# Banded QK scores of a dilated attention: from products on VectorE to dense blocks on TensorE

## The chip, the cores and the metric

The kernel runs on one core of a Trainium2 chip. The metric is the device time of one execution in microseconds. The core has TensorE (PE, matrix products into PSUM), VectorE (DVE), ScalarE (ACT), GpSimd (POOL) and SyncE (SP), whose queue issues nearly all DMAs here. Each engine takes its instructions in order; semaphores tie them together.

## The reference

Two branches work on the same x (2048 positions, 1024 channels) and are mixed by a gate. Branch A is an attention with 32 heads of 32 channels in which every position looks at itself and at the seven positions 2, 4, ... 14 before it. Branch B is a gated MLP whose gate is mixed over positions by a 2048 x 2048 matrix.

```python
g = sigmoid((x * gate_w).sum(-1, keepdims=True))

# A: W = 8 keys per query, dilation 2
q, k, v = split(x @ wqkv)                      # 32 heads x 32 channels
idx = pos[:, None] - 2 * arange(8)[None, :]    # keys of a position; idx < 0 is masked
logits = einsum('bhsd,bhswd->bhsw', q, k[idx]) * 32 ** -0.5
a = einsum('bhsw,bhswd->bhsd', softmax(where(idx >= 0, logits, -1e9)), v[idx]) @ wo

# B
z = gelu(x @ w_in)                             # 2048 x 3584
z1, z2 = z[..., :1792], layernorm(z[..., 1792:])
b = (z1 * (w_sp @ z2 + b_sp[:, None])) @ w_out

out = g * a + (1 - g) * b
```

## The kernel before

One arena in SBUF is cut into regions that are used again from stage to stage (Z, X, A, CD, EF by their offsets); the tile framework sets the semaphores and orders each engine's instructions from the program order and from priorities (`tc.high_priority()` lifts a piece). PSUM is eight banks of 512 words a partition, handed out in turn by `next_bank`. The stages, in the order in which TensorE does them:

1. Start: x is brought in transposed (`xT`), and a first quarter of z2 (`z2_tile(i, 0)`, L214) with the gate's column is made. `g_d` and `og_d` carry the gate through DRAM.
2. QKV: for each of eight groups of four heads, 16 tiles `j` (L249). A tile takes the positions j, j+16, j+32, ... as its rows, so its weights are read from `xT` at a stride, and gives q, k and v of the group side by side, 384 columns. ScalarE copies it to a stage slot (L252), and every fourth tile three DMAs write q, k and v to `q_d`, `k_d` and `v_d`. The weights of v are first reordered on ScalarE (L244).
3. Attention, VectorE only, group by group: q, k and v come back from DRAM so that a partition holds 16 consecutive positions and the 14 before them (`q_t`, `k_t`, `v_t`). In two halves of eight positions, q times the eight shifted k (L273, 8192 products a partition), four halving adds over the 32 channels (L276) and a last one into `att_L` (L277), then the mask (L278), the softmax in 32 bits (L279 to L290) with the exponential on ScalarE (L283), the products with v (L295) and three halving adds over the eight keys (L297 to L299). Every second group is written to `o_d`.
4. The other three quarters of z2 (L214), its layer norm (L311 to L322), then z1 (L381), which goes to `z1_d` over two slots (`z1s_slots`).
5. Spatial product: the 2048 x 2048 product as two halves of seven `spatial_quad` each, and within these seven products of half size in the manner of Strassen, each of eight matmuls (L391); the sums of operands are VectorE's. The two halves of w_sp are read by DMA transposes (`load_raw`, eight each; SP's line L187). The second half's place, `raw_slots[1]`, is at `A_OFF`, where `q_t`, `k_t`, `v_t`, `prod` and `obuf` of the attention lie.
6. Output: eight `out_quad`, seven products of eleven matmuls (L391), from `zg_d` and `o_d`.

The framework lets the attention on VectorE run beside stages 2, 4, 5 of TensorE; work of the spatial stage with high priority goes between its instructions.

Of the kernel before, what the change touches and what calls it, by code (L numbers as in the profile page):

```python
# [28 lines left out]
NEG = -1.0e30  # L29
EPS = 1e-5  # L30
SCALE = DH ** -0.5
WGS = 4 * KT * C
# [19 lines left out]
def kernel(  # L52
# [32 lines left out]
    def reg(off, n):  # L85
        return arena[:, off:off + n]

    q_d = dpool.tile([NG, S, C], BF, name="q_d")
    k_d = dpool.tile([NG, S + 16, C], BF, name="k_d")
# [9 lines left out]
    mask = sm.tile([P, 2 * W * 8 * HG], BF, name="mask")  # L99
    nc.gpsimd.memset(mask[:], 0.0)  # L100
    m5 = mask[:].rearrange("p (a w j h) -> p a w j h", a=2, w=W, j=8, h=HG)
    for jh in range(2):
        for w in range(W):
            n = min(8, max(0, 14 - 2 * w - 8 * jh))
            if n > 0:
                nc.gpsimd.memset(m5[0:1, jh, w, 0:n, :], NEG)
# [14 lines left out]
    att_L = sm.tile([P, 2 * W * 8 * HG], F32, name="att_L")  # L121
    att_m = sm.tile([P, 2, 4, 32], F32, name="att_m")
    att_r = sm.tile([P, 2, 1, 32], F32, name="att_r")
    att_A = sm.tile([P, 2 * W * 8 * HG], BF, name="att_A")

# [6 lines left out]
    q_t = reg(A_OFF, NJ * C)  # L132
    k_t = reg(A_OFF + 2048, NJJ * C)
    v_t = reg(A_OFF + 2048 + 3840, NJJ * C)
    prod = reg(A_OFF + 2048 + 7680, W * 8 * C)
    obuf = reg(A_OFF + 2048 + 7680 + 8192, NJ * 2 * C).rearrange("p (j c) -> p j c", j=NJ)
    w2 = reg(CD_OFF, KT * W2P).rearrange("p (k c) -> p k c", k=KT)
    w2_off = [0, 480, 480 + ZC, 480 + 2 * ZC]
    stage_slots = [reg(CD_OFF + 14848 + r * 1536, 1536).rearrange("p (j c) -> p j c", j=4) for r in range(3)]
    wg_slots = [reg(EF_OFF + r * WGS, WGS).rearrange("p (t k c) -> p t k c", t=4, k=KT) for r in range(3)]  # L140
    junk = reg(EF_OFF + 3 * WGS, FH)
# [17 lines left out]
    def load_wg(g, dma):  # L159
        wgt = wg_slots[g % 3]  # L160
        dma(wgt[:, 3, :, :], wq_v[:, :, 2 * D + g * C:2 * D + (g + 1) * C])
        dma(wgt[:, 0, :, :], wq_v[:, :, g * C:(g + 1) * C])
        dma(wgt[:, 1, :, :], wq_v[:, :, D + g * C:D + (g + 1) * C])
# [8 lines left out]
    load_wg(0, lambda o, i: chained(nc.sync.dma_start(o, i)))  # L172
    load_wg(1, lambda o, i: chained(nc.sync.dma_start(o, i)))
    for t_d in (k_d, v_d):
        chained(nc.sync.dma_start(bass.AP(tensor=t_d.tensor, offset=t_d.offset, ap=[[16, P], [(S + 16) * C, NG], [1, 16]]), zeros[:]))
# [34 lines left out]
    def z2_tile(i, c):  # L210
        N = ZC + 1 if c == 0 else ZC
        ps = next_bank()
# [18 lines left out]
    sync.dma_start(g_att[:], bass.AP(tensor=g_d.tensor, offset=g_d.offset, ap=[[NJ, P], [1, NJ]]))  # L231

    stg = 0
    for g in range(NG):
        wgt = wg_slots[g % 3]
        if g > 1:
            load_wg(g, sync.dma_start)
        vdst = wgt[:, 2, :, :].rearrange("p k (d h) -> p k d h", d=DH, h=HG)
        vsrc = wgt[:, 3, :, :].rearrange("p k (h d) -> p k d h", h=HG, d=DH)
        if g == 0:  # L240
            nc.scalar.copy(vdst[:, 0:4], vsrc[:, 0:4])
            nc.vector.tensor_copy(vdst[:, 4:8], vsrc[:, 4:8])
        else:
            nc.scalar.copy(vdst, vsrc)  # L244
        for j in range(NJ):
            ps = next_bank()
            for kt in range(KT):
                lhsT = _sub_ap(xT_flat, kt * S + j, [[NJ, P]])
                nc.tensor.matmul(ps[:, 0:3 * C].rearrange("p (t c) -> p t c", t=3), lhsT, wgt[:, 0:3, kt, :],  # L249
                                 start=(kt == 0), stop=(kt == KT - 1))  # L250
            st = stage_slots[stg % 3]
            nc.scalar.copy(st[:, j % 4, :], ps[:, 0:3 * C])  # L252
            if j % 4 == 3:
                j0 = j - 3
                dq = bass.AP(tensor=q_d.tensor, offset=q_d.offset + (g * S + j0) * C, ap=[[NJ * C, P], [C, 4], [1, C]])
                dk = bass.AP(tensor=k_d.tensor, offset=k_d.offset + (g * (S + 16) + 16 + j0) * C, ap=[[NJ * C, P], [C, 4], [1, C]])
                dv = bass.AP(tensor=v_d.tensor, offset=v_d.offset + (g * (S + 16) + 16 + j0) * C, ap=[[NJ * C, P], [C, 4], [1, C]])
                sync.dma_start(dq, st[:, :, 0:C])
                sync.dma_start(dk, st[:, :, C:2 * C])
                sync.dma_start(dv, st[:, :, 2 * C:3 * C])  # L260
                stg += 1

    L = att_L
    L4 = L[:].rearrange("p (a w n) -> p a w n", a=2, w=W, n=32)
    A4 = att_A[:].rearrange("p (a w n) -> p a w n", a=2, w=W, n=32)
    for g in range(NG):
# [3 lines left out]
        for jh in range(2):  # L270
# [4 lines left out]
            for half in (16, 8, 4, 2):  # L275
                nc.vector.tensor_tensor(pv[:, :, 0:half], pv[:, :, 0:half], pv[:, :, half:2 * half], ALU.add)  # L276
# [29 lines left out]
    for c in range(1, 4):  # L306
        sync.dma_start(w2[:, :, w2_off[c]:w2_off[c] + ZC], win_v[:, :, FH + ZC * c:FH + ZC * (c + 1)])
    for i in range(16):
        for c in range(1, 4):
            z2_tile(i, c)  # L310
# [314 lines left out]
```

## Time and profile before

| | us |
|---|---|
| median of 2 runs (766.35 to 766.77) | 766.56 |
| the profiled execution | 767.75 |
| its span, first to last instruction | 765.7 |
| busy TensorE / VectorE / ScalarE | 683.0 / 527.4 / 247.9 |
| mean granted TensorE clock | 0.958 |
| moved by DMA | 108.15 MB |

The profile is of one execution. A group of its lines is a line of the kernel, an engine, an operation and its operands, the count, the busy time and the mean of one in ns, then the engine's idle time just before them and what ended it. A matmul's shown duration overlaps the next one's, so tiles are better read from the distance of their starts. A stage's length is read from TensorE's timeline: 37.7 us start, 185.2 QKV, 80.4 rest of z2, about 101 z1, 361.4 spatial and output.

### The profile page before, as it was taken

The page shows a single profiled execution, that of the slowest core. Times are in us where ns is not written, and L with a number is a line of the kernel's source. Part 1 is how long each engine was busy: PE and PEld are TensorE (multiplying, and loading weights), DVE is VectorE, ACT ScalarE, POOL GpSimd, SP SyncE. Part 2 cuts the span into 40 slices and gives each one's busy share as a digit, 9 for nine tenths or more (in the row PEclk, how much of TensorE's full clock was granted, in tenths as well). Part 3 has the DMA queues.
Part 4 walks back from the last instruction along what each step waited for, and adds up shares of the span by engine and source line. Part 5 has one row for each costly group of instructions (what it writes and reads, how often), then busy time and mean ns, then how long its engine had stood idle before and what let it go on. Part 6 is the DMA issues. An engine that isn't in the chain of part 4 may idle for free.

```text
span 765.7 us, 8952 instructions
## 1 busy us (share of the span) xinstructions
PE 683.0 (89%) x3416; PEld 384.6 (50%) x3416; DVE 527.4 (69%) x559; ACT 247.9 (32%) x502; POOL 13.3 (2%) x23
## 2 busy tenths in 40 slices
PE   5996999999798997989996999910999989999998
PEld 3584888888674553434442444400344434444443
DVE  1000399999999999999999999991587667433300
ACT  3442545252354957325341122200121111222121
POOL 0000000000000011100000000000000000000000
PEclk9997999999999999999998999965899999999999
DMA  9999966646673230993664223289544568964111
GB/s 216 181 97 151 288 162 152 173 103 171 160 188 135 90 96 2 206 306 117 190 212 134 55 71 95 70 250 203 110 110 134 147 133 173 206 134 101 46 42 42
DMA packets 246362, 108.15 MB, mean 141 GB/s; under 512 B 206896, under 2 KB 237616, under 8 KB 246320
## 3 DMA queue, kind: packets, MB, share of 16 engines
q1 hardware_dynamic: 245280, 107.59, 58.0%
q8 instruction: 26, 0.43, 0.3%
q10 hardware_dynamic: 1040, 0.00, 0.1%
q14 instruction: 16, 0.13, 0.1%
HBM read 56.11 MB, written 35.73 MB: 120 GB/s over the span
## 4 chain that ended last, share of the span: by engine, by line
DVE 42%; PE 32%; DMA 10%; SPq 9%; issue 4%; ACT 2%; POOL 1%; DVEq 0%; ACTq 0%; POOLq 0%
DVE arena L276 8%; DVE arena L273 7%; DVE arena L295 6%; PE bank_68 L391 4%; PE bank_72 L391 4%; PE bank_74 L391 4%; DVE arena L297 4%; PE bank_71 L391 4%; SPq L187 4%; PE bank_67 L391 4%; PE bank_70 L391 4%; SPq L171 3%; DMA g_d<-g_s 2%; PE bank_69 L391 2%; DMA arena<-z_d 2%
## 5 line engine op out<-in xcount | busy, mean ns | idle before, releaser
L391 PEld LDWEIGHTS <-arena 128*128 128x128 f16 (+1 forms) x1400 | 138.5, 99 | 219.2 <-issue 51.0
L249 PEld LDWEIGHTS <-arena 128*128 128x128 bf16 x1024 | 148.1, 145 | 36.1 <-issue 17.2
L273 DVE TENSOR_TENSOR arena<-arena 128x8192 bf16<-128x8192 bf16 x16 | 70.8, 4426 | 46.6 <-DMA arena<-k_d 46.3
L391 PE MATMUL bank_71<-arena 128*128 128x512 bf16 x200 | 49.2, 391 | 34.1 <-DMA arena<-in_B_w_sp_dram 34.1
L214 PEld LDWEIGHTS <-arena 128*128 128x128 bf16 x512 | 50.9, 100 | 55.8 <-issue 11.1
L276 DVE TENSOR_TENSOR arena<-arena 128x4096 bf16<-128x4096 bf16 (+1 forms) x64 | 77.6, 1212 | 1.4
L381 PEld LDWEIGHTS <-arena 128*128 128x128 bf16 x448 | 43.8, 98 | 56.9 <-issue 4.4
L295 DVE TENSOR_TENSOR arena<-arena,att_A 128x8192 bf16<-128x8192 bf16 x16 | 70.8, 4424 | 0.4
L391 PE MATMUL bank_70<-arena 128*128 128x512 f16 x200 | 48.7, 388 | 5.0 <-DVE arena L420 5.0
L391 PE MATMUL bank_72<-arena 128*128 128x512 f16 x200 | 48.5, 388 | 3.4 <-ACT bank_72 L399 2.7
L391 PE MATMUL bank_68<-arena 128*128 128x512 f16 x200 | 48.3, 386 | 2.4 <-DVE arena L421 2.4
L391 PE MATMUL bank_67<-arena 128*128 128x512 bf16 x200 | 48.5, 387 | 0.0
L391 PE MATMUL bank_74<-arena 128*128 128x512 f16 x200 | 46.7, 379 | 1.7 <-DVE arena L363 1.7
L420 DVE TENSOR_TENSOR arena<-arena 128x1024 f16<-128x1024 f16 (+2 forms) x30 | 17.9, 602 | 36.2 <-DMA arena<-zg_d 13.8
L297 DVE TENSOR_TENSOR arena<-arena 128x4096 bf16<-128x4096 bf16 x16 | 36.6, 2290 | 0.3
L399 ACT COPY bank_72<-bank_71 128x512 f32<-128x512 f32 x11 | 6.3, 570 | 84.4 <-PE bank_71 L391 71.0
L249 PE MATMUL bank_71<-arena 128*128 128x384 bf16 x128 | 24.7, 338 | 7.4 <-ACT arena L252 7.4
L422 DVE TENSOR_TENSOR arena<-arena 128x1024 f16<-128x1024 f16 (+2 forms) x30 | 17.7, 602 | 16.6 <-PE bank_72 L391 8.4
L249 PE MATMUL bank_67<-arena 128*128 128x384 bf16 x128 | 24.7, 338 | 4.3 <-ACT arena L252 4.3
L311 ACT ACTIVATE arena<-arena 128x1792 bf16<-128x1792 bf16 x16 | 27.2, 1700 | 0.4
L283 ACT ACTIVATE att_L<-att_L 128x512 f32<-128x512 f32 x8 | 5.0, 630 | 65.1 <-DVE att_L L282 65.1
L249 PE MATMUL bank_69<-arena 128*128 128x384 bf16 x128 | 23.4, 326 | 1.5 <-ACT arena L252 1.5
(167 smaller groups left out, 904.1 us busy)
## 6 DMA issues: line engine op xcount, KB each, us to landing
arena<-k_d SPq DMA_DIRECT2D x8, 960.0 KB, 6.7
arena<-v_d SPq DMA_DIRECT2D x8, 960.0 KB, 5.4
z_d<-arena SPq DMA_DIRECT2D x14, 512.0 KB, 5.9
arena<-z_d SPq DMA_DIRECT2D x28, 256.0 KB, 3.3
zg_d<-arena SPq DMA_DIRECT2D x56, 128.0 KB, 2.2
arena<-zg_d SPq DMA_DIRECT2D x32, 224.0 KB, 3.2
arena<-in_A_wqkv_dram SPq DMA_DIRECT2D x24, 256.0 KB, 4.6
q_d<-arena SPq DMA_DIRECT2D x32, 128.0 KB, 5.2
```

Source lines behind the costliest of these rows:

```text
L171: chained(nc.sync.dma_start_transpose(xT[:, :, i * P:(i + 1) * P], x2[i * P:(i + 1) * P, :]))
L187: inst = _orig_dmat(*a, **k)
L214: nc.tensor.matmul(ps[:, 0:N], xT[:, kt, i * P:(i + 1) * P], w2[:, kt, w2_off[c]:w2_off[c] + N], start=(kt == 0), stop=(kt == KT - 1))
L249: nc.tensor.matmul(ps[:, 0:3 * C].rearrange("p (t c) -> p t c", t=3), lhsT, wgt[:, 0:3, kt, :], start=(kt == 0), stop=(kt == KT - 1))
L273: nc.vector.tensor_tensor(prod.rearrange("p (w j c) -> p w j c", w=W, j=8, c=C), in0, in1, ALU.mult)
L276: nc.vector.tensor_tensor(pv[:, :, 0:half], pv[:, :, 0:half], pv[:, :, half:2 * half], ALU.add)
L295: nc.vector.tensor_tensor(prod.rearrange("p (w j d h) -> p w j d h", w=W, j=8, d=DH, h=HG), in0, in1, ALU.mult)
L297: nc.vector.tensor_tensor(p3[:, 0:4, :], p3[:, 0:4, :], p3[:, 4:8, :], ALU.add)
L311: nc.scalar.activation(junk, z2[:, i, :], ACT.Square, accum_out=s2[:, i:i + 1])
L381: nc.tensor.matmul(ps[:], w1[:, kt, (f % 4) * P:(f % 4 + 1) * P], xT[:, kt, 512 * c:512 * (c + 1)], start=(kt == 0), stop=(kt == KT - 1))
L391: nc.tensor.matmul(bank[:], lhsT, rhs, start=(start and m == 0), stop=(stop and m == n - 1), skip_group_check=True)
L420: nc.vector.tensor_tensor(s_out[0], a21, a22, ALU.add)
```

## The change

The scores q·k are no longer made on VectorE. Positions are split by parity, so that the eight keys of a query are eight neighbours within its parity.

- q and k are made transposed (`qk_tile`: channels on partitions, 512 positions a tile) and copied to `qT` and `kT` with even and odd positions apart. v is made for four groups at once (`v_tile`, 512 columns) and reordered in the copy.
- A block is 128 queries of one parity against 135 keys (their own 128 and the 7 before). For each of four heads it is one matmul with 32 channels of contraction; the four heads stand in four row tiles of the array (`tile_position`) and go to banks 4 to 7. Six `band_set` of two or three blocks make a group's 16 blocks. ScalarE copies each head's bank to 16 bits, heads innermost, and a DMA writes the whole rows (135 x 4 values, 1080 bytes) to `band_d`. The part in front of position 0 is filled with -60000 once.
- In `attend`, two DMAs read back, for every query, the 8 x 4 values of its band (64 bytes); the address moves by a row and one key from query to query (`BR + HG`), and that takes the diagonal out. The softmax is in 16 bits. The products with v stay on VectorE.
- Order: q and k of group g+1 (and v in groups 0 and 3, and twelve tiles of z2 in the last) are put between the six sets of group g; these use banks 0 to 3 (`low_bank`). The loads of w2 and of the first two w1 are issued earlier.

```diff
+KW = P + W - 1
+BR = KW * HG
+BS = P * (BR + HG)
...
-    q_d = dpool.tile([NG, S, C], BF, name="q_d")
-    k_d = dpool.tile([NG, S + 16, C], BF, name="k_d")
+    band_d = [dpool.tile([16, BS], F16, name=f"band_d{g}") for g in range(NG)]
...
-    load_wg(0, lambda o, i: chained(nc.sync.dma_start(o, i)))
-    load_wg(1, lambda o, i: chained(nc.sync.dma_start(o, i)))
+    load_wqk(0, lambda o, i: chained(nc.sync.dma_start(o, i)))
+    for hf in range(2):
+        chained(nc.sync.dma_start(wv[:, :, 512 * hf:512 * hf + 512], wq_v[:, :, 2 * D + 512 * hf:2 * D + 512 * hf + 512]))
+        load_wqk(1 + hf, lambda o, i: chained(nc.sync.dma_start(o, i)))
...
-    sync.dma_start(g_att[:], bass.AP(tensor=g_d.tensor, offset=g_d.offset, ap=[[NJ, P], [1, NJ]]))
+    for e in range(2):
+        sync.dma_start(g_att[:, 8 * e:8 * e + 8].rearrange("p (j o) -> p j o", o=1),
+                       bass.AP(tensor=g_d.tensor, offset=g_d.offset + e, ap=[[NJ, P], [2, 8], [1, 1]]))
...
+    def qk_tile(g, t, c):
+        ps = low_bank()
+        w = wqk_slots[g % 4]
+        for kt in range(KT):
+            nc.tensor.matmul(ps[:], w[:, t, kt, :], xT[:, kt, 512 * c:512 * (c + 1)], start=(kt == 0), stop=(kt == KT - 1))
+        dst = (qT_slots, kT_slots)[t][g % 2]
+        nc.scalar.copy(dst[:, :, 256 * c:256 * (c + 1)], ps[:].rearrange("p (n e) -> p e n", e=2))
+
+    def v_tile(hf, j):
...
+        nc.scalar.copy(_sub_ap(st, (j % 4) * 512, [[C, 4], [1, HG], [HG, DH]]), ps[:].rearrange("p (g h d) -> p g h d", g=4, h=HG))
...
+    band_sets = [(0, 8, 2), (1, 1, 3), (9, 1, 3), (4, 1, 3), (12, 1, 3), (7, 8, 2)]
...
+    def band_set(g, x):
+        first, step, n = band_sets[x]
+        qt, kt_ = qT_slots[g % 2], kT_slots[g % 2]
...
+            st = band_slots[band_at[0] % 3]
...
+        for m in range(n):
+            e, b = divmod(first + m * step, 8)
+            for h in range(HG):
+                hp = slice(DH * h, DH * (h + 1))
+                nc.tensor.matmul(banks[4 + h][:, m * KW + lo:(m + 1) * KW], qt[hp, e, P * b:P * (b + 1)],
+                                 kt_[hp, e, P * b - (W - 1) + lo:P * (b + 1)], start=True, stop=True,
+                                 tile_position=(DH * h, 0), skip_group_check=True)
+        for h in range(HG):
+            src = banks[4 + h][:, 0:n * KW].rearrange("p (m k) -> p m k", m=n)[:, :, lo:KW]
+            nc.scalar.copy(st[:, 0:n, lo:KW, h], src)
+        bd = band_d[g]
+        dst = bass.AP(tensor=bd.tensor, offset=bd.offset + first * BS, ap=[[BR, P], [step * BS, n], [1, BR]])
+        sync.dma_start(dst, st[:, 0:n].rearrange("p m k h -> p m (k h)"))
+
+    def attend(g):
+        L = att_L[g % 2]
...
+        for e in range(2):
+            sync.dma_start(L[:, 256 * e:256 * e + 256].rearrange("p (j x) -> p j x", j=8),
+                           bass.AP(tensor=bd.tensor, offset=bd.offset + 8 * e * BS, ap=[[8 * (BR + HG), P], [BR + HG, 8], [1, W * HG]]))
...
-            nc.vector.tensor_tensor(prod.rearrange("p (w j c) -> p w j c", w=W, j=8, c=C), in0, in1, ALU.mult)
-            pv = prod.rearrange("p (n d) -> p n d", d=DH)
-            for half in (16, 8, 4, 2):
-                nc.vector.tensor_tensor(pv[:, :, 0:half], pv[:, :, 0:half], pv[:, :, half:2 * half], ALU.add)
-            nc.vector.tensor_tensor(L[:, jh * 256:(jh + 1) * 256], pv[:, :, 0], pv[:, :, 1], ALU.add)
-        nc.vector.tensor_tensor(L[:], L[:], mask[:], ALU.add)
...
+    for g in range(NG):
+        if g + 3 < NG:
+            load_wqk(g + 3, sync.dma_start)
+        main = []
+        if g in (0, 3):
+            main += [lambda j=j, hf=g // 3: v_tile(hf, j) for j in range(NJ)]
+        if g + 1 < NG:
+            main += [lambda t=t, c=c, g=g + 1: qk_tile(g, t, c) for t in range(2) for c in range(4)]
+        else:
+            main += [lambda c=c, i=i: z2_tile(i, c, low_bank) for i in range(4) for c in range(1, 4)]
+        done = 0
+        for x in range(6):
+            band_set(g, x)
+            upto = (x + 1) * len(main) // 6
+            for m in range(done, upto):
+                main[m]()
+            done = upto
+        attend(g)
...
+    load_w1(0)
+    load_w1(1)
     load_raw(0)
```

In the changed kernel the copies out of the bands are L280, those of q and k L245 and of v L253, the band matmuls L275, those of q and k L243 and of v L250, the exponential L300.

## The prediction

> **What bounds the kernel now.** I read the page's busy times and slices first, then the busy time by stage, then TensorE's one long wait and its releaser, then the costliest groups. In the slices a digit is tenths busy in 19.1 us.
>
> ```profile
> PE 683.0 (89%) x3416; PEld 384.6 (50%) x3416; DVE 527.4 (69%) x559; ACT 247.9 (32%) x502; POOL 13.3 (2%) x23
> PE   5996999999798997989996999910999989999998
> DVE  1000399999999999999999999991587667433300
> ```
>
> TensorE (PE) is the busiest, but VectorE (DVE) is solid from 82 to 520 us. The stages, by time (stretch, length, then busy time and count of each engine):
>
> ```profile
> 37.70:222.90 185.20, 171.97 (x1032) 148.64 (x1031) 129.39 (x96) 72.45 (x154) 0.00 (x0) 0.96 0.74 162
> 222.90:303.30 80.40, 73.32 (x379) 37.35 (x378) 76.06 (x80) 56.33 (x124) 4.94 (x2) 0.98 0.31 97
> 303.30:405.80 102.50, 98.68 (x458) 44.58 (x456) 97.15 (x80) 41.92 (x76) 6.53 (x2) 1.00 0.68 193
> 405.80:520.00 114.20, 86.86 (x386) 38.19 (x384) 110.20 (x131) 17.79 (x30) 0.00 (x0) 0.90 0.41 115
> 520.00:555.00 35.00, 18.37 (x70) 7.47 (x71) 11.14 (x8) 2.88 (x5) 0.00 (x0) 0.71 0.77 165
> 555.00:615.00 60.00, 60.00 (x279) 27.19 (x278) 42.07 (x59) 10.63 (x19) 0.00 (x0) 1.00 0.48 125
> 615.00:765.70 150.70, 144.48 (x661) 64.88 (x659) 58.51 (x100) 29.86 (x52) 0.00 (x0) 0.99 0.50 111
> ```
>
> These are QKV (L249), the rest of z2 (L214), z1 (L381), then the spatial and output products (L391). TensorE is full in all but two, 405.8 to 555, where it idles some 44 of 149 us. The cause is one chain, read from three engines' timelines and the list of waits:
>
> ```profile
> 518.13 0.69 DVE L299 TENSOR_TENSOR arena<-arena 128x1024 bf16<-128x1024 bf16 x1
> 518.85 0.59 SPq L182 DMA_DIRECT2D o_d<-arena  x1
> 519.49 22.91 SPq L187 DMA_TRANSPOSE arena<-in_B_w_sp_dram  x8
> PE bank_71 L391 <- DMA arena<-in_B_w_sp_dram: 34.1, 1, 34.1
> ```
>
> The last attention instruction ends at 518.8. The second half of w_sp (load_raw(1)) is laid over the attention's buffers, so its eight transposes start only then, and TensorE waits 34.1 us for them. So attention on VectorE (43.5 us a group, from 132.17, where a group's first L273 starts, to 175.70, where the next one's does; eight groups) bounds the middle, TensorE's own work the rest.
>
> **TensorE without waits, before.** The timeline's starts give a tile of eight matmuls as 1.30 us at 384 columns, 1.52 at 448 and 1.73 at 512; eleven of 512 take 2.375. z1 is 56 x 1.73 = 96.9. The spatial stage is 14 x 7 x 1.73 = 169.5 and the output 8 x 7 x 2.375 = 133.0, together 302.5, where the trace has 361.4 (404.3 to 765.7): 59 lost.
>
> **Part 1: attention on VectorE, removed.** The costliest groups:
>
> ```profile
> L273 DVE TENSOR_TENSOR arena<-arena 128x8192 bf16<-128x8192 bf16 x16 | 70.8, 4426 | 46.6 <-DMA arena<-k_d 46.3
> L276 DVE TENSOR_TENSOR arena<-arena 128x4096 bf16<-128x4096 bf16 (+1 forms) x64 | 77.6, 1212 | 1.4
> L295 DVE TENSOR_TENSOR arena<-arena,att_A 128x8192 bf16<-128x8192 bf16 x16 | 70.8, 4424 | 0.4
> L244 ACT COPY arena<-arena 128x1024 bf16<-128x1024 bf16 x7 | 14.1, 2013 | 2.0 <-DMA arena<-in_A_wqkv_dram 2.0
> L252 ACT CAST arena<-bank_71 128x384 bf16<-128x384 f32 x16 | 7.9, 496 | 31.6 <-DMA v_d<-arena 25.9 <-PE bank_71 L249 5.7
> ```
>
> L273, L276, L277 (16 x 0.61) and L278 (8 x 0.69) go: 70.8 + 77.6 + 9.7 + 5.5 = 163.6 us. What stays of a group is the value product, 2 x (4.42 + 2.29 + 1.23 + 0.69 + four gaps of 0.035) = 17.5, and the softmax, 5.05 in 32 bits (153.11 to 158.16). In 16 bits I take 4.2, since L276's 512 and 1024 elements already run at half the price of the 32-bit rows. So a group takes 21.7 us (22.6 if 16 bits give nothing). Eight are 174 against 348.
>
> **Part 2: TensorE's projections, moved.** QKV was 128 x 1.30 = 166.4. Now 64 q and k tiles and 32 v tiles of 512 columns take 96 x 1.73 = 166.1, no change. Twelve z2 tiles (18.2 us) move into the stage; 36 (54.7) stay behind it.
>
> **Part 3: band matmuls, added.** 8 groups x 16 blocks x 4 heads = 512 of 135 columns, in 48 sets. No row has this shape. By L381's rate (216 ns per 512 columns) one takes 57 ns, I take 60: 30.7 us. If the four heads truly overlap it is a quarter, 7.7. The worst row is the start's transposes, 128 columns with a weight load each, every 107 ns: 54.8. I stay with 60: right behind those transposes a z2 tile still took 3.21 us against 1.68 for the later ones, so they ran in a slow start.
>
> They also use another tiling of the array (tile_position), so each set changes it twice. No row shows such a change. At the least it costs nothing; at the most the array empties each time, and as a L249 matmul is shown for 326 ns while the next starts after 162, that is 164 ns: 96 x 0.164 = 15.7. I take the middle, 8, since in the sets with one tile between them TensorE waits for banks anyway. The Trainium skill (TensorEngine Tiling (Array Packing), Tiling Modes, Key Properties) says that changing the tiling mode drains TensorE; no row here shows a switch. By the rule the sum has up to all of the 15.7, 8 more; by the row, where matmul follows matmul without a break, none of it, 8 less.
>
> **Part 4: copies out of PSUM on ScalarE (ACT).** Per group 16 of 405 and 8 of 270 elements; before, L252 moved 384 in 496 ns, one every 0.375 us. By that, a set's four end 3 x 0.395 + 0.51 = 1.7 us after they start. The next set (own banks per head) can't finish before: 0.1 wait, nine matmuls 0.54, 0.3 until the copy starts, so 2.6 us a set against 1.73 + 0.72 = 2.45 on TensorE. That costs 0.15 x 4 sets x 6 groups, 4 us. The copies of q, k and v tiles (0.57 each by L401's 512 elements, the v ones permuted) lie under matmul tiles of 1.73 and cost nothing; without that cover the 32 of v are 18 us. Band copies write at a distance of 8 bytes. L244, which reads at 64 bytes, takes 2013 ns for 1024 and L241 1082 for 512, so 1.8 ns an element: 405 would be 0.88. I take L252's price, because the source is PSUM as there.
>
> The Trainium skill (SBUF — State Buffer, Door 1: The DMA port swizzle) says accesses keep full speed with two or more in a 16-byte line. L244 has one, and pays; the new writes have two, so by the rule they are free and by the row 24 x 0.35 = 8 us of ScalarE a group dearer. No row here has two.
>
> **Part 5: the way through DRAM.** A group writes 2.2 MB of bands (six DMAs) where q and k wrote 1.0 and read 1.5. At some 22 us a group, with values (0.96), weights (0.5) and outputs (0.5), that is 4.2 MB / 22 = 190 GB/s; 40:80 us of the start ran at a share of 0.98, 200:240 moved 159 GB/s at 0.57. So it fits. SP issues eleven DMAs a group there at 0.4 to 0.6 us, before 18. The mask's memsets (POOL, 1.9 us in the first 40) and the earlier w1 loads I cost at nothing, because TensorE has z2 work then; bare, one w1 load is 8.1 us. The hand-over per group is write (zg_d's 128 KB land in 2.2 us, z_d's 512 KB in 5.9: 4 for 270 KB), wait and issue 1, read of 2 x 1024 pieces of 64 bytes (896 pieces of zg_d land in 3.2: 3.5), issue 1.5 in all: 10 us, then 1.5 of max and subtract. Ends: 6 by two rows of 2.2, or 16 if the read takes the 9.6 us that g_att's did.
>
> Here is the new wait. The exponential (L300) stands in ScalarE's queue in front of band copies, and TensorE waits for those banks. In the changed kernel's instruction order exp of group 0 stands after group 1's first set (8.7 us after its last band copy), of group 3 after four q/k copies (7.5), others two or three sets on (10 to 13). Ready at 11.5, or when VectorE has finished the group before. Group 0 waits 11.5 + 1.28 for the function table + 0.63 - 8.7, some 4; group 3 11.5 + 0.63 - 7.5, again 4; following both queues the same way through the others (period 20.5 on TensorE, 21.7 on VectorE) gives 1, 1, 0, 0 and 3 for groups 1, 2, 4, 5 and 6, the last with two table loads. SP also blocks: L(4)'s read stands behind an o_d write that waits for attend(3); I count it inside these. Add 2 at the start, where g_att waits for g_d (17.5 us to land) in front of the first band and value writes.
>
> **Sum.** Stage: 166.1 + 18.2 + 30.7 + 8 + 4 + 13 + 2 = 242. It runs from 37.7 to 279.7. Rest of z2, 54.7 + 2: to 336.4. VectorE ends attention near 315, so both halves of w_sp load from there: 16 transposes x 2.5 us on SP (519.49 above: 22.9 for eight), to some 360. The z1 writes stand behind them; two z1 slots and eight banks cover 28 us of TensorE from 336, so 6 are lost: 96.9 + 6. Spatial and output 302.5, and 7 at their two joints (before: 5.0 and 2.4 at 405 to 417, 2.7 at 620), and 3.5 at the end (L565 and the last store). That is 336.4 + 102.9 + 313 = 752.3 of span. The profiled execution took 767.75 with a span of 765.7, 2.05 around it; the median of the runs is 766.56. So **755 us**, of itself 738 to 770.
>
> **Rivals.** *A, the array overlaps and the hand-over is short.* Four heads at once save 23, but then the copies bind (2.4 against 2.6), so 12; short hand-overs save the 9 of groups 0, 1 and 3: 755 - 21 = 734. For it: the tiles name separate row groups and banks. Against: ScalarE.
>
> *B, slower: ScalarE's copies become the bound.* Place: L280. At 0.88 instead of 0.39 us, a group's ScalarE work is 16 x 0.88 + 8 x 0.62 + 8 x 0.57 + 0.6 = 24.2, and with the 0.9 us of turn-round in four sets 28: 7.5 above my 20.5 in six groups, 45: 800. It decides beyond 782 from about 0.7 us a copy. For it L244; against it L252.
>
> *C, the hand-over is long.* At 16 us each of seven groups waits 4 to 6 more: 785 to 797; at 13, some 775. For it the many 64-byte pieces; against, DMA is not full after 120 us.
>
> *D, that the 34 us stay.* Nothing else holds the attention's buffers; no more than 3 in 100, within C.
>
> **How the numbers follow.** Forecast 0.50 (0.20 of it below 751), A 0.20, B 0.17, C 0.13 (half of it within 2%). Two per cent of 766.56 is 15.3 us, about what a measurement of this kernel can tell from no change: faster, under 751.2, 0.20 + 0.20 = 0.40; same 0.30 + 0.07 = 0.37; slower, over 781.9, 0.17 + 0.06 = 0.23. The range goes from A, 730, to short of B's full price, 793, leaving some 2 in 10 out.
>
> **What would show it.** Right: no wait of L391 for w_sp, TensorE full from 340 us, VectorE's attention ending near 315, L280 at 0.5 us, the band matmuls 60 ns apart, ScalarE waiting for VectorE at L300. Wrong: L280 over 0.7 (B), the att_L read over 8 us to landing (C), a stage ending after 300 us, or a new idle stretch at z1 over 15 us.

## Result and the profile after: slower, and ScalarE's copies are the reason

| | us |
|---|---|
| median of 2 runs of the changed kernel (785.79 to 787.84) | 786.82 |
| median before | 766.56 |
| ratio, with its 95% interval | 1.026 (1.021 to 1.032) |
| the profiled execution / its span | 787.84 / 785.7 |

The change costs 20 us where 12 less had been forecast. In the forecast, rival B had named this outcome and its place, L280. The page's busy times and slices (a digit is now tenths of 19.6 us):

```profile
PE 720.4 (92%) x3672; PEld 335.9 (43%) x3672; DVE 361.6 (46%) x462; ACT 402.9 (51%) x649; POOL 6.0 (1%) x13
PE   5997868799778887899999999999999999999998
DVE  1000027487192756795120008667888478332310
ACT  3456968999699889998523332212211121222221
```

VectorE was relieved as meant (527.4 to 361.6 us). But ScalarE rose from 247.9 to 402.9, and its 8s and 9s (slices 5 to 19, 78 to 373 us) lie over the stretch in which TensorE shows 6 to 8 (slices 4 to 17, with two 9s). From slice 18 on TensorE is full. By stage (stretch, length, then busy time and count of PE, PEld, DVE, ACT, POOL, granted clock, DMA share, GB/s):

```profile
37.70:105.20 67.50, 59.58 (x320) 31.45 (x318) 0.25 (x2) 47.57 (x59) 0.00 (x0) 0.92 0.84 148
105.20:292.50 187.30, 152.55 (x897) 67.64 (x896) 112.44 (x110) 165.27 (x215) 0.00 (x0) 0.89 0.47 135
292.50:380.50 88.00, 79.53 (x450) 40.09 (x450) 57.73 (x69) 80.32 (x156) 4.00 (x3) 0.98 0.49 132
380.50:478.40 97.90, 96.78 (x449) 43.79 (x448) 14.13 (x18) 34.07 (x59) 1.01 (x1) 1.00 0.61 154
478.40:785.70 307.30, 302.70 (x1401) 136.91 (x1399) 174.81 (x256) 60.11 (x105) 0.00 (x0) 1.00 0.47 117
```

These are the start with v and group 0, groups 1 to 6, the last group and the rest of z2, z1, and the spatial and output products. In the second row TensorE lacks 35 of 187 us, while ScalarE is busy 88% of it. The last row took 361.4 us before. Of the 54 us that it lost, 34.1 are the wait for w_sp: among TensorE's waits there is none for it any more. The costliest groups of ScalarE, shapes apart:

```profile
L280 ACT CAST arena<-bank_73 128x405 f16<-128x405 f32 x32 | 37.9, 1186 | 0.0
L253 ACT CAST arena<-bank_69 128x512 bf16<-128x512 f32 x8 | 11.6, 1450 | 0.0
L245 ACT CAST arena<-bank_67 128x512 bf16<-128x512 f32 x16 | 9.6, 598 | 13.2 <-PE bank_67 L243 13.2
```

All three copy PSUM into 16 bits. L245 reads PSUM at a distance of 8 bytes and writes in a row: 598 ns for 512. L253 and L280 read in a row and write at 8 bytes: 1450 ns for 512, 1186 for 405. So the price follows the writing side. ScalarE's timeline in the middle, and what TensorE did then (start, duration):

```profile
216.10 0.84 ACT L280 CAST arena<-bank_74 128x256 f16<-128x256 f32 x1
216.67 0.69 ACT L245 CAST arena<-bank_68 128x512 bf16<-128x512 f32 x1
217.49 1.07 ACT L280 CAST arena<-bank_71 128x405 f16<-128x405 f32 x1
218.29 1.18 ACT L280 CAST arena<-bank_72 128x405 f16<-128x405 f32 x1
219.19 1.18 ACT L280 CAST arena<-bank_73 128x405 f16<-128x405 f32 x1
220.10 1.18 ACT L280 CAST arena<-bank_74 128x405 f16<-128x405 f32 x1
221.05 0.65 ACT L245 CAST arena<-bank_69 128x512 bf16<-128x512 f32 x1
```

```profile
208.45 1.90 PE L243 MATMUL bank_68<-arena 128*128 128x512 bf16 x8
215.27 0.21 PE L275 MATMUL bank_71<-arena 32*128 32x135 bf16 x1 [4.92 <-ACT arena L280]
215.84 0.27 PE L275 MATMUL bank_72<-arena 32*128 32x135 bf16 x1 [0.35 <-ACT arena L280]
216.41 0.27 PE L275 MATMUL bank_73<-arena 32*128 32x135 bf16 x1 [0.31 <-ACT arena L280]
216.99 0.27 PE L275 MATMUL bank_74<-arena 32*128 32x135 bf16 x1 [0.31 <-ACT arena L280]
217.42 3.60 PE L243 MATMUL bank_69<-arena 128*128 128x512 bf16 x8
```

```profile
217.40:221.00 3.60, 3.60 (x14) 1.10 (x12) 3.60 (x1) 3.51 (x4) 0.00 (x0) 0.50 0.22 77
```

The starts of successive copies are 0.80, 0.90 and 0.91 us apart: 0.91 is the sustained price, 2.25 ns an element. The four heads' matmuls, which want to start together, start one by one as L280 frees their banks. TensorE also runs slower here: after its stop of 4.92 us the granted clock was 0.50 from 217.4 to 221.0 us, and a tile of q or k took 3.53 us from its start to the next set instead of 1.73. ScalarE was busy 3.51 of these 3.60 us, so it remained the bound there.

A group's period is read from the first matmuls of its first set: 105.23, 138.28, 162.79, 208.22, 238.22, 265.17 and 292.54 us for groups 1 to 7. Five of the six steps have q and k alone: 33.1, 24.5, 30.0, 27.0 and 27.4, mean 28.4. Rival B's sum had said 28, the forecast 20.5. (The step of 45.4 also holds the 16 v tiles.)

Against the forecast's span of 752.3 us, z1 starts at 380.5 instead of 336.4 (+44.1), takes 97.9 instead of 102.9 (-5.0), and the rest takes 307.3 instead of 313 (-5.7): together +33.4, the span of 785.7.

### The profile page after: what moved, and what is told of

It is laid out like the page before. It is cut to its first block, busy times and chain, and to the rows that moved or that the text cites. A ratio compares the mean times of both kernels' runs of the same rounds, so it can differ in the third digit from the quotient of the medians.

```text
span 785.7 us, 9516 instructions
## 1 busy us (share of the span) xinstructions
PE 720.4 (92%) x3672; PEld 335.9 (43%) x3672; DVE 361.6 (46%) x462; ACT 402.9 (51%) x649; POOL 6.0 (1%) x13
## 4 chain that ended last, share of the span: by engine, by line
PE 55%; SPq 2%; ACT 1%; DMA 1%; DVE 0%; issue 0%; ACTq 0%; DVEq 0%
PE bank_72 L435 6%; PE bank_71 L435 5%; PE bank_67 L435 5%; PE bank_68 L435 5%; PE bank_74 L435 5%; PE bank_70 L435 5%; PE bank_73 L435 3%; PE bank_69 L435 3%; SPq L183 2%; PE bank_71 L425 1%; PE bank_69 L425 1%; PE bank_67 L425 1%; PE bank_72 L425 1%; PE bank_68 L425 1%; PE bank_73 L425 1%; PE bank_74 L425 1%
## 5 line engine op out<-in xcount | busy, mean ns | idle before, releaser
L243 PEld LDWEIGHTS <-arena 128*128 128x128 bf16 x512 | 50.9, 104 | 67.7 <-issue 20.2
L210 PEld LDWEIGHTS <-arena 128*128 128x128 bf16 x512 | 50.3, 99 | 49.8 <-issue 5.0
L315 DVE TENSOR_TENSOR arena<-arena,att_A 128x8192 f16<-128x8192 bf16 x16 | 70.7, 4421 | 0.2
L425 PEld LDWEIGHTS <-arena 128*128 128x128 bf16 x448 | 43.8, 98 | 54.1 <-issue 1.4
L280 ACT CAST arena<-bank_73 128x405 f16<-128x405 f32 (+2 forms) x48 | 51.9, 1081 | 0.0
L280 ACT CAST arena<-bank_74 128x405 f16<-128x405 f32 (+2 forms) x48 | 51.8, 1079 | 0.0
L280 ACT CAST arena<-bank_72 128x405 f16<-128x405 f32 (+2 forms) x48 | 51.7, 1076 | 0.0
L250 PEld LDWEIGHTS <-arena 128*128 128x128 bf16 x256 | 36.6, 145 | 28.0 <-issue 10.5
L280 ACT CAST arena<-bank_71 128x405 f16<-128x405 f32 (+2 forms) x48 | 47.7, 993 | 0.3
L435 PE MATMUL bank_72<-arena 128*128 128x512 f16 x200 | 46.8, 379 | 1.0 <-ACT bank_72 L443 1.0
L435 PE MATMUL bank_70<-arena 128*128 128x512 f16 x200 | 46.9, 379 | 0.0
L435 PE MATMUL bank_71<-arena 128*128 128x512 bf16 x200 | 46.8, 379 | 0.0
L435 PE MATMUL bank_67<-arena 128*128 128x512 bf16 x200 | 46.8, 379 | 0.0
L435 PE MATMUL bank_68<-arena 128*128 128x512 f16 x200 | 46.8, 379 | 0.0
L435 PE MATMUL bank_74<-arena 128*128 128x512 f16 x200 | 46.8, 379 | 0.0
L482 DVE TENSOR_TENSOR arena<-arena 128x2048 f16<-128x2048 bf16 x14 | 17.1, 1222 | 62.5 <-DMA arena<-z_d 62.2
L275 PEld LDWEIGHTS <-arena 32*128 32x128 bf16 x512 | 14.5, 93 | 70.5 <-issue 70.5
L464 DVE TENSOR_TENSOR arena<-arena 128x1024 f16<-128x1024 f16 (+2 forms) x30 | 17.8, 601 | 46.9 <-PE bank_74 L435 19.8
L243 PE MATMUL bank_70<-arena 128*128 128x512 bf16 x128 | 39.1, 459 | 0.0
L317 DVE TENSOR_TENSOR arena<-arena 128x4096 f16<-128x4096 f16 x16 | 36.6, 2290 | 0.4
```

What stands on the lines that cost most here:

```text
L210: nc.tensor.matmul(ps[:, 0:N], xT[:, kt, i * P:(i + 1) * P], w2[:, kt, w2_off[c]:w2_off[c] + N], start=(kt == 0), stop=(kt == KT - 1))
L243: nc.tensor.matmul(ps[:], w[:, t, kt, :], xT[:, kt, 512 * c:512 * (c + 1)], start=(kt == 0), stop=(kt == KT - 1))
L250: nc.tensor.matmul(ps[:], _sub_ap(xT_flat, kt * S + j, [[NJ, P]]), wv[:, kt, 512 * hf:512 * hf + 512], start=(kt == 0), stop=(kt == KT - 1))
L275: nc.tensor.matmul(banks[4 + h][:, m * KW + lo:(m + 1) * KW], qt[hp, e, P * b:P * (b + 1)], kt_[hp, e, P * b - (W - 1) + lo:P * (b + 1)], ...
L280: nc.scalar.copy(st[:, 0:n, lo:KW, h], src)
L315: tt(prod.rearrange("p (w j d h) -> p w j d h", w=W, j=8, d=DH, h=HG), in0, in1, ALU.mult)
```

## Experiments

All edits are of the changed kernel. "Before" was run beside each; its median was 766.6 to 771.9 us from session to session, so ratios are compared.

### The band copies write in a row

```diff
-            nc.scalar.copy(st[:, 0:n, lo:KW, h], src)
+            nc.scalar.copy(st[:, 0:n, h, lo:KW], src)
```

The staging slots are laid out head by head; bytes, DMAs and matmuls stay, so the scores read back are not the right ones, and only the time counts here.

> The band copies (L280) write each head's 135 values side by side instead of 8 bytes apart; bytes, DMAs and their pieces stay, so the values read back are those of other keys (the kernel's output is not the reference's). Theory S (the write distance makes ScalarE's copies slow, and they pace the band stage): copies of 405 elements fall from 1.17 to about 0.5 us, a group's period from 26 to the 22 us of VectorE, six groups x 4 and some 7 in the two value groups, so about 756 us. Rival M (the copy out of PSUM to 16 bits is slow whatever the distance): copies stay at 1.1 and the time at 787. Rivals T (band matmuls and switches of tiling) and H (the way through DRAM) also leave 787, T and H with copies at 0.5.

Measured: 740.12 us, ratio 0.966 (0.961 to 0.971). The copy:

```profile
L280 ACT CAST arena<-bank 128x405 f16<-128x405 f32 x128 | 55.8, 530 | 0.1
```

z1 starts at 331.1 instead of 380.5. So the distance of the writes costs 47 us, more than the loss, and without it the change would be a gain. It went lower than the theory's number, since other terms of the sum had been priced too high (below).

### One distance for each head

```diff
+        def dist(d):
+            return _sub_ap(flat, d * lo, [[d * KW, n], [d, KW - lo]])
+        nc.scalar.copy(dist(1), srcs[0])
+        nc.scalar.copy(dist(2), srcs[1])
+        nc.scalar.copy(dist(3), srcs[2])
+        nc.scalar.copy(dist(4), srcs[3])
```

> Each head's band copy writes at another distance: head 0 side by side, heads 1, 2 and 3 at 2, 3 and 4 elements of 16 bits (the values land over each other, so the output is not the reference's). Theory S: 0.5 us at distance 1 and 1.1 at distance 4; by the Trainium skill (SBUF, Door 1: The DMA port swizzle) all four lie within two a 16-byte line and are equal at 0.5, by a price per piece 2 and 3 already cost 1.1. Rival M: all four at 1.1.

Measured, at distances of 2, 4, 6 and 8 bytes (L285 to L288):

```profile
L285 ACT CAST arena<-bank 128x405 f16<-128x405 f32 x32 | 17.1, 533 | 0.1
L286 ACT CAST arena<-bank 128x405 f16<-128x405 f32 x32 | 20.1, 628 | 0.9
L287 ACT CAST arena<-bank 128x405 f16<-128x405 f32 x32 | 27.0, 845 | 1.1 <-PE bank L276 0.3
L288 ACT CAST arena<-bank 128x405 f16<-128x405 f32 x32 | 34.2, 1070 | 0.9
```

The price climbs with the distance: 4 bytes cost 95 ns more, 8 bytes twice the row. One run took 764.3 us, between the two ends, as its mean copy of 769 ns is. The rule weighed in the forecast (the Trainium skill, SBUF — State Buffer, Door 1: The DMA port swizzle: full speed with two or more accesses in a 16-byte line) would have the last line as cheap as the first; at 8 bytes two accesses do share a line, and the measurement decides against it.

### Every band matmul twice

```diff
-        for m in range(n):
+        for m in list(range(n)) * 2:
```

> Every band matmul (L275) is done twice, 512 more of them, nothing else changed. Theory S (ScalarE paces): 0 to 5 us more, 787 to 792, as they lie under its copies. Rival T (TensorE's band work is what was mis-sized, 60 ns each or more): 20 to 31 us more.

Measured: 793.02 us, ratio 1.034 (1.029 to 1.039) against 1.026 (1.021 to 1.032). The two intervals overlap, so the 512 added matmuls cost some 6 us, hardly to be told from nothing (theory S had 0 to 5). The 20 to 31 that a bound on TensorE would give are excluded.

### The columns of v's weights reordered once

```diff
+                nc.vector.tensor_copy(wvr[hf][:, k, :].rearrange("p (g d h) -> p g d h", g=4, d=DH),
+                                      wv[:, k, 512 * hf:512 * hf + 512].rearrange("p (g h d) -> p g d h", g=4, h=HG))
...
-        nc.scalar.copy(_sub_ap(st, (j % 4) * 512, [[C, 4], [1, HG], [HG, DH]]), ps[:].rearrange("p (g h d) -> p g h d", g=4, h=HG))
+        nc.scalar.copy(_sub_ap(st, (j % 4) * 512, [[1, 512]]), ps[:])
```

Sixteen copies on VectorE take the distance out of the 32 v copies (L253).

> VectorE, idle at the start, reorders the value weights once (16 copies), so that the value copies (L253 before) write side by side: 1.45 to 0.57 us, 32 of them. Theory S: some 20 us less of ScalarE in groups 0 and 3, of which the start's DMA wait hides part: 772 to 779. Rival (these groups wait for DMA and TensorE only): 784 to 787.

Measured: 778.45 us, ratio 1.017 (1.010 to 1.023). L253 falls from 1.44 to 0.62 us, and z1 starts 9.2 us earlier (371.3). The interval just overlaps the changed kernel's (1.021 to 1.032), so the gain of some 8 us rests on the trace as well, and on the version with pairs below, where the same edit (with the next one, which alone changes nothing) brings as much. The same cause at a second place: the forecast had put these copies under the matmul tiles at no cost.

### The gate read in a row

```diff
-    for e in range(2):
-        sync.dma_start(g_att[:, 8 * e:8 * e + 8].rearrange("p (j o) -> p j o", o=1),
-                       bass.AP(tensor=g_d.tensor, offset=g_d.offset + e, ap=[[NJ, P], [2, 8], [1, 1]]))
...
+            if g == 0 and x == 3:
+                sync.dma_start(g_raw[:], bass.AP(tensor=g_d.tensor, offset=g_d.offset, ap=[[NJ, P], [1, NJ]]))
+                nc.vector.tensor_copy(g_att[:].rearrange("p (e j) -> p e j", e=2), g_raw[:].rearrange("p (j e) -> p e j", e=2))
```

> The gate is read back in 128 pieces of 64 bytes and put in order on VectorE, where the changed kernel reads it in 2048 pieces of 4 bytes and SP takes 4.8 us to issue them and 10.8 for the weight loads behind. Theory: the wait of ScalarE for v_d (8.2 us) at the start goes: 778 to 783 us. If ScalarE's slow value copies hide it: 785 to 787.

Measured: ratio 1.027 (1.023 to 1.032), no change. ScalarE's one long wait at the start, for a v slot to be written, is 8.7 us here and 8.2 in the changed kernel. So the small pieces of the gate's read are not its cause. The read itself isn't cleared: it still holds SP for 8.1 us ahead of the first v write (4.8 in the changed kernel). In both, SP also spends 11 to 14 us in that stretch issuing loads of weights; that these hold the writes back was not tried by itself.

### Two heads side by side

```diff
+HP = 2
+HQ = HG // HP
+BS = P * (BR + HP)
...
-            nc.scalar.copy(st[:, 0:n, lo:KW, h], src)
+            nc.scalar.copy(st[:, 0:n, h // HP, lo:KW, h % HP], src)
...
+                           bass.AP(tensor=bd.tensor, offset=bd.offset + 8 * e * BS, ap=[[8 * (BR + HP), P], [BR + HP, 8], [KW * HP, HQ], [1, W * HP]]))
```

The distance is 4 bytes, and the read takes 32-byte pieces; the computation is whole.

> A band row holds two heads side by side twice instead of four interleaved, so ScalarE writes 4 bytes apart, and the read takes 4096 pieces of 32 bytes a group instead of 2048 of 64; the whole computation is done. Theory S (0.62 us at this distance): the stage as with contiguous copies plus a little, 742 to 750 us. Rival H (the way through DRAM: smaller pieces make the hand-over the bound): 760 or more.

Measured: 759.56 us, ratio 0.985 (0.981 to 0.990), less gain than the theory's. The copy and the read:

```profile
L283 ACT CAST arena<-bank 128x405 f16<-128x405 f32 x128 | 67.8, 651 | 0.2
att_L<-band_d SPq DMA_DIRECT2D x16, 64.0 KB, 3.8
```

### One head by itself

The same with `HP = 1`: copies in a row, the read in 16-byte pieces. (In the expectation, e6 is the version before this one and e7 this one.)

> Each head has its own 135 values side by side in the band row; ScalarE writes contiguously, and the read takes 8192 pieces of 16 bytes a group; the whole computation is done. At 28 ns a piece (the mean of all packets in the changed kernel) 49152 more pieces are 86 us of all 16 DMA engines on top of some 55% in a stage of 240: so theory S alone says 740, and with DMA as the next bound 755 to 790; between e6 and e7 the piece, not the copy, decides.

Measured: 770.47 us, ratio 0.999 (0.996 to 1.001). ScalarE's price is gone, but others came:

```profile
L283 ACT CAST arena<-bank 128x405 f16<-128x405 f32 x128 | 55.6, 526 | 0.2
L313 DVE TENSOR_TENSOR att_A<-att_L,att_r 128x256 f16<-128x256 f16 x16 | 19.2, 1390 | 0.3
att_L<-band_d SPq DMA_DIRECT2D x16, 64.0 KB, 5.7
```

The read lands after 5.7 us (3.0 in the changed kernel). VectorE pays for the transposition that ScalarE no longer makes: its write to `att_A`, now of single elements 64 bytes apart, takes 1390 ns against 378 with two in a row (pairs), 16 us over the 16. Not all of that need be the write: the operand that is repeated over the eight keys is read one by one as well, and with that alone, writing in a row, the subtraction (L302) rose from 424 to 691 ns for 512 elements. TensorE's z1 starts at 353.9, 23 us later than with writes in a row. The way there is ScalarE's queue: at the exponential it waits 33.2 us for VectorE and the read (with writes in a row 15.4), and TensorE waits 27.2 us for its banks (12.7). How much of this is the read and how much VectorE was not taken apart. The time lies in the 755 to 790 expected of a bound on DMA, but the DMA engines' share was 0.66 from 104 to 272 us (0.61 in the same groups with writes in a row), so they were not full. The distance had been moved, not removed.

### Pairs, v's weights and the gate together, and pairs with 64-byte pieces

> Full computation: bands written by pairs of heads (4-byte writes, 32-byte pieces in the read), the columns of v's weights reordered once on VectorE so that the copies of v tiles write contiguously, and the gate read contiguously and reordered on VectorE. Theory S (ScalarE's strided copies are what the change pays): the 405-element copies stay at 0.65 us, the v copies fall from some 1.4 to 0.6 us, and as that took 8 us off the changed kernel, another 4 to 9 go from the pair version, ratio 0.973 to 0.980 to the kernel before. Rival H (with pairs the hand-over through DRAM and VectorE bind, and no ScalarE time counts any more): as the pair version, 0.983 to 0.988.

> The pair version (4-byte writes, 405-element copies at 0.65 us), but the read takes 64-byte pieces in a row as the contiguous version did, so it fetches half of its heads' scores from wrong places: the same number of bytes in half as many pieces. It splits what lies between the pair version (ratio 0.985) and the contiguous one (0.966). Copies theory: on the line between the contiguous version (0.53 us a copy, 740) and the changed kernel (1.17, 787), some 73 us for each us of copy, 0.65 us gives 749, and 32-byte pieces cost the rest: ratio 0.973 to 0.980, att_L read 3.0 us. Pieces theory: all of the difference is the read's, ratio 0.966. Neither: the read's pieces cost nothing and it stays at 0.985.

The second one's edit:

```diff
-                           bass.AP(tensor=bd.tensor, offset=bd.offset + 8 * e * BS, ap=[[8 * (BR + HP), P], [BR + HP, 8], [KW * HP, HQ], [1, W * HP]]))
+                           bass.AP(tensor=bd.tensor, offset=bd.offset + 8 * e * BS, ap=[[8 * (BR + HP), P], [BR + HP, 8], [1, W * HG]]))
```

Measured: 0.976 (0.973 to 0.979) for the first, as theory S says, with the v copies at 0.59 us. The second: 0.970 (0.967 to 0.973). So of the 15 us between pairs (0.985) and writes in a row (0.966), the pieces of the read are 12 (0.015 x 771) and the last 0.12 us a copy only 3, hardly to be told from nothing. The copies theory had given them 9: its straight line does not hold below some 0.65 us a copy, where ScalarE seems to stop being the bound. Most of the 12 lie ahead of z1, which starts at 332.4 instead of 341.9, and ScalarE's waits at the exponential are 12.0 us instead of 17.0. Landing, 3.1 against 3.8 us, is 0.7 a group; what else of the pieces costs was not taken apart.

### The distance on PSUM's side: one copy for four heads

```diff
-    banks = [psum.tile([P, 512], F32, name=f"bank{b}") for b in range(8)]
+    banks = [psum.tile([P, 512], F32, name=f"bank{b}") for b in range(4)]
+    heads = psum.tile([P, HG, 512], F32, name="heads")
+    banks += [heads[:, h, :] for h in range(HG)]
...
-        nc.scalar.copy(_sub_ap(st, (j % 4) * 512, [[C, 4], [1, HG], [HG, DH]]), ps[:].rearrange("p (g h d) -> p g h d", g=4, h=HG))
+        nc.scalar.copy(_sub_ap(st, (j % 4) * 512, [[C, 4], [HG, DH], [1, HG]]), ps[:].rearrange("p (g h d) -> p g d h", g=4, h=HG))
...
-        for h in range(HG):
-            src = banks[4 + h][:, 0:n * KW].rearrange("p (m k) -> p m k", m=n)[:, :, lo:KW]
-            nc.scalar.copy(st[:, 0:n, lo:KW, h], src)
+        src = heads[:, :, 0:n * KW].rearrange("p h (m k) -> p m k h", m=n)[:, :, lo:KW, :]
+        nc.scalar.copy(st[:, 0:n, lo:KW, :], src)
```

The same elements go to the same places, walked in the order of the destination.

> Full computation, the layout of the changed kernel in DRAM (four heads innermost, 64-byte pieces in the read), but the distance is moved from the write to the read: one copy for a set walks the four heads' banks (each element 2 KB from the last in PSUM) and writes in a row; the v copies too read at a distance and write in a row. Theory S (what costs is the distance of the 16-bit writes; q and k copies, which read PSUM at 8 bytes, took about what a plain copy does): with 0.87 ns an element (530 ns for 405, 412 for 270) and 0.18 fixed, a copy of 1620 elements takes 1.6 us, and the v copies 0.6 instead of 1.4; the stage is TensorE's, and the time is that of the contiguous version or some us less, ratio 0.955 to 0.967. Rival P (a distance costs the same on the side of PSUM, or a step from bank to bank does): at 2.6 ns an element, as between 405 and 270 at the full distance, a set's copy takes 4.2 us, and the ratio is 1.02 or above.

Measured: 768.02 us, ratio 0.993 (0.990 to 0.997), neither theory's number. The copies are theory S's:

```profile
L281 ACT CAST arena<-heads 128x1620 f16<-128x1620 f32 x32 | 48.4, 1513 | 0.4 <-PE heads L277 0.2 <-ACT arena L247 0.2
L255 ACT CAST arena<-bank 128x512 bf16<-128x512 f32 x32 | 18.1, 589 | 33.5 <-PE bank L252 19.0 <-DMA v_d<-arena 13.3 <-remote 1.1
```

A set's 1620 elements take 1.51 us where the four copies took some 4 x 0.91, and the v copies 0.59. Each element lies 2 KB from the last in PSUM, and it costs nothing to be seen. z1 starts at 328.0, 52 us before the changed kernel's. (Rival P's 2.6 ns an element is too much: with one distance for each head, the copies at 8 bytes took 770 ns for 270 elements and 1070 for 405, so 2.2 an element and some 3.7 us for a set. It did not take that either.) But from there to the end it takes 441 us (changed kernel: 405). Two windows within the spatial stage, and z1's one stop:

```profile
540.00:580.00 40.00, 35.25 (x153) 15.39 (x154) 29.10 (x39) 4.01 (x7) 0.00 (x0) 0.96 0.33 82
580.00:620.00 40.00, 34.77 (x145) 14.81 (x147) 24.33 (x33) 6.81 (x12) 0.00 (x0) 0.91 0.52 134
```

```profile
355.25 0.60 ACT L428 ACTIVATE arena<-heads 128x512 bf16<-128x512 f32 x1 [12.53 <-DMA z_d<-arena]
355.90 3.57 PE L426 MATMUL heads<-arena 128*128 128x512 bf16 x8 [10.36 <-ACT arena L428]
```

ScalarE's activation of z1 (L428) waits until a write of z1 has left its slot, and TensorE waits for ScalarE.

### The banks set free, and z1's writes on another queue

```diff
+    head_pool.__exit__(None, None, None)
+    tail_pool = ctx.enter_context(tc.tile_pool(name="tail", bufs=1, space=bass.MemoryType.PSUM))
+    banks[4:8] = [tail_pool.tile([P, 512], F32, name=f"bank{b}") for b in range(4, 8)]
...
-        sync.dma_start(z1_d[:, :, f * 512:(f + 1) * 512].rearrange("c p t -> p c t"), z1s)
+        nc.scalar.dma_start(z1_d[:, :, f * 512:(f + 1) * 512].rearrange("c p t -> p c t"), z1s)
```

The first three lines (with `heads` in a pool of its own) make the first version, all of it the second.

> The version with one copy for four heads, with one thing more: the four banks, which there stay one PSUM tile of 2048 words to the end, become four tiles of one bank again after the attention. There the stage ended at 328 us, the earliest of all, but from there to the end it took 441 us, against 410 in the contiguous version. Theory T (the common tile ties products of different banks together in z1 and the spatial stage, as waits between PE, ACT and DVE for 'heads'): the spatial windows are full again (39.9 instead of 34.8 to 39.5 of 40 us), and it takes some 18 to 25 us off: 744 to 751 where that took 769, ratio 0.963 to 0.975; the 10 us that z1 waits for its writes behind the w_sp transposes stay. Rival O (the order of instructions, which also changes with the fewer copies, is what costs): same as that version, 0.990 to 0.997.

> As the version before it in this call, and the writes of z1 are issued from ScalarE's queue instead of SP's, where sixteen w_sp transposes (40 us of issue) stand in front of them. Theory Z (z1's two slots wait for writes that SP holds back, the 6 us of the prediction, 10 in the trace with one copy for four heads): TensorE has no stop within z1, 8 to 12 us less than without this edit, ratio 0.950 to 0.962, and below the contiguous version's 0.966. Rival A (ScalarE's queue pays for issuing, or the writes collide with the transposes in the DMA engines): the stop moves to a later place and no more than 3 us are gained.

Measured: ratio 0.958 (0.953 to 0.962), some 736 us, for the first: the common PSUM tile had cost 0.036 x 769 = 27 us, and theory T was short by a little. For the second 729.88 us, ratio 0.949 (0.946 to 0.951), the best of all: the edit brought 0.0087 x 769 = 7 us, against 8 to 12 expected. That these 7 are z1's stop is not shown: in the first version's trace, taken at a granted clock of 0.943 instead of 0.988, TensorE stops in z1 for only 1.9 us. The second version's stages, and its z1 on TensorE without a stop:

```profile
102.00:242.50 140.50, 127.46 (x880) 60.47 (x896) 107.22 (x107) 86.55 (x107) 0.00 (x0) 0.96 0.62 175
540.00:580.00 40.00, 39.75 (x182) 18.05 (x185) 26.36 (x36) 6.54 (x12) 0.00 (x0) 1.00 0.53 137
322.80 96.86 PE L431 MATMUL bank<-arena 128*128 128x512 bf16 x439
```

Groups 1 to 6 take 140.5 us where the changed kernel took 187.3, and ScalarE is busy 62% of it.

## Why the prediction was wrong, point by point

**The step that failed** is in part 4: "I take L252's price, because the source is PSUM as there." It set a band copy at 0.51 us and one every 0.395. Measured: 1.18 (405 elements, three of the four banks) and one every 0.91, and writing in a row, which brings the copy to 0.53, takes 47 us off the kernel. L252 and L244 differed in two things, source and distance, and the price was chosen by the source. The four-heads copy settles it: with PSUM as the source and 2 KB between elements, 0.93 ns an element; with PSUM as the source and 8 bytes between writes, 2.25 sustained. L244's 1.8 was the nearer row (it has its distance in SBUF, though on the reading side), and even it was too low. B's threshold, beyond 782 us from about 0.7 us a copy, was too low: with a mean of 0.77 (one distance for each head) the one run took 764.3. Copies of 0.65 cost next to nothing: the time (pairs with 64-byte pieces) is within 3 us of that at 0.53. Nor would the forecast's number have come out with its own price: at 0.53 us a copy the kernel took 740, 15 less than 755, so that the other terms were off as well, as follows.

**The v copies**, in the same part, "cost nothing": 1.44 us each instead of 0.57, and 8 to 9 us of time.

**Part 3 was too dear.** 512 matmuls at 60 ns and 8 us of switches, 38.7 together. In the best version's timeline sets stand between tiles so:

```profile
195.39 0.36 PE L278 MATMUL heads<-arena 32*128 32x135 bf16 x12
195.69 1.90 PE L246 MATMUL bank<-arena 128*128 128x512 bf16 x7
197.54 0.36 PE L278 MATMUL heads<-arena 32*128 32x135 bf16 x12
197.84 1.90 PE L246 MATMUL bank<-arena 128*128 128x512 bf16 x8
199.67 0.30 PE L278 MATMUL heads<-arena 32*128 32x135 bf16 x8
199.91 2.33 PE L246 MATMUL bank<-arena 128*128 128x512 bf16 x10
```

From the start of one tile to the next, over a set of twelve, 197.84 - 195.69 = 2.15 us pass, over a set of eight 199.91 - 197.84 = 2.07. A tile alone takes 1.73, so a set costs 0.42 or 0.34 with both changes of tiling: 32 x 0.42 + 16 x 0.34 = 18.9 us, 20 less than the sum had. An estimate splits them: four more matmuls add 0.08 (0.06 by the times from a set's start to the next tile's, 0.30 and 0.24), so four take some 0.07 us, the 128 fours 9 us instead of 30.7, and the two changes are what is left, 0.2 a set or 10 us in all instead of 8. So the four row tiles do run together, and the matmuls are the term that was too dear. The Trainium skill's drain at a change of mode (TensorEngine Tiling (Array Packing), Tiling Modes, Key Properties) fits the 0.1 us a change; the sum's upper bound was 0.164.

**Part 1 was right.** Group 0 on VectorE runs from 111.79 to 133.33 us: 21.5, forecast 21.7.

**Part 5 was right.** Group 0's last band write is issued at 101.31 and VectorE starts at 111.79: 10.5 us, forecast 10. The read lands in 2.7 to 3.3 us (3.5), the writes in 2.8 to 5.6 (4). Rival C did not occur in the changed kernel; at 5.7 us (16-byte pieces) it began to count.

**The wait at L300** showed rarely: 5.1 us once and 3.5 at group 0's table load, not 13. ScalarE was mostly late itself. In the best version, with ScalarE free, it waits there 14.0 us in all, and TensorE 14.8 for the bands' banks: the term was about right for a kernel in which the copies don't bind.

**The start**, 2 us, was 8, the wait for the v slot's write; why is left open, except that it is not the small pieces of the gate's read.

**z1's 6 us** had the right mechanism but not here: z1 started so late (380.5) that the w_sp transposes (366.4 to 405.1) ended before its cover of 28 us did. In the version with writes in a row TensorE did stop, after 27.8 us of z1 as forecast, for 3.6, and with one copy for four heads for 10.4; taking the writes from SP's queue brought 7 us there.

**w_sp** came as forecast, and spatial and output took 307.3 us where the forecast had 313.

**Rival B's 800** was 13 too high, 11.6 of them in the span, and that is not in the copies. With its 45 us z1 would have started at 336.4 + 45 = 381.4; it started at 380.5. The rest are z1's 5.0 and the last stages' 5.7. That the start of z1 fits to a microsecond is partly luck: the start cost 6 more, and the step with the v tiles was 45.4 where B makes it 20.5 + 16 x 1.73 + 7.5 = 55.7. The period of 28 is luck in part, too. ScalarE was busy 24.0 to 25.5 us in each of the five steps with q and k alone, as B's 24.2 had it. But only the step from 138.3 to 162.8 us, at a granted clock of 1.00, was as short as that; the others, with clocks of 0.79 to 0.89 and in two of them a wait at L300 of 3.5 or 5.1 us, took 27.0 to 33.1, and B's 0.9 us of turn-round in four sets was not measured by itself.

## What to carry to other kernels

When a copy must interleave or transpose 16-bit data on its way out of PSUM, walk it in the order of the destination and let PSUM take the distance: here that was 1.51 us against some 3.6 for the same 1620 elements. Give the common PSUM tile up when the stage is over: kept to the end, it cost 27 us. An operation that no row of the old profile shows should be priced by the row that shares its access pattern in SBUF, and when two rows differ by more than the point at which an engine becomes the bound, that rival deserves more than a sixth. An engine that looks idle on the average (ScalarE was at 32%) must be summed up again by stage once work is added to one stage alone.

## What the hardware showed that was not expected

- ScalarE's 16-bit writes from PSUM: 533 ns for 405 elements in a row, 628 at a distance of 4 bytes, 845 at 6, 1070 at 8 (a mean of up to 1186 a bank in the changed kernel). Its reads of PSUM at 8 bytes took 586 ns for 512 in the version with one copy for four heads (L247), the same as a copy that reads in a row there (L600), and at 2 KB, over four banks in one instruction, 1513 for 1620.
- VectorE's 16-bit writes of single elements 64 bytes apart were also dear: 1390 ns for 256 against 378 for pairs of them, part of it perhaps the repeated operand.
- In the skewed read 1024 pieces of 64 bytes land in 3.0 to 3.1 us, 2048 of 32 in 3.8, 4096 of 16 in 5.7. From 64 to 32 bytes the kernel lost 12 us.
- Twelve matmuls of 135 columns in four row tiles took, with both changes of tiling, 0.42 us of TensorE's time; three 512-column matmuls of the whole array take 0.65.
- After a stop of TensorE of 4.92 us the granted clock was 0.50 for some 3.5 us (217.4 to 221.0), and a tile took 3.53 us instead of 1.73.
